# Softmax sums of 32 attention heads in PE column tiles, their inverses replicated by DMA, and three heads woven in the source

## Chip, cores and metric

The kernel runs on one core of one Trainium2 chip. The time is device microseconds (us) of one execution; each kernel is executed several times and the median is quoted, with the lowest and highest. TensorE's mean granted clock was 0.978 to 0.985 unless another value is given. TensorE is called PE below, VectorE DVE, ScalarE ACT, GpSimd POOL.

## The reference, cut to what matters

Four layers follow one another: A, B, A, B. Layer A is a two-dimensional Fourier filter; the change does not touch it. Layer B is attention with a memory: 64 segments of 32 positions, each attending to 8 memory rows and itself, 32 heads of 128, model width 640.

```python
for s in range(n_seg):                                   # 64 segments
    xs = x[:, s * seg_len:(s + 1) * seg_len, :]
    h = jnp.concatenate([mem, xs], axis=1)               # 8 + 32 rows
    q, k, v = (jnp.einsum('btd,dhe->bhte', h, W) for W in (Wq, Wk, Wv))
    scores = jnp.einsum('bhqe,bhke->bhqk', q, k) * scale # masked
    p = softmax(scores)
    o = jnp.einsum('bhte,hed->btd', jnp.einsum('bhqk,bhke->bhqe', p, v), Wo)
    mem = o[:, :M, :]                                    # memory of the next segment
    outs.append(o[:, M:, :])
x = x + _B_ref(_layernorm(x), B_mem0, B_Wq, B_Wk, B_Wv, B_Wo, seg_len)
```

## The kernel before

The kernel guesses the memory of every segment, computes all segments at once, and checks the guess afterwards (a slower pass exists for a failed check; it does not run on these inputs). So layer B is a loop over 32 heads of large matmuls: the projections Q, K, V, then scores, exponentials, sums, values. The queries of a head (2119 columns) are cut into five groups `g_` of at most 502 columns, each with its own PSUM bank. This is the part that the change replaces, shortened with `...`:

```python
def scores(h):
    for i, part in enumerate(st.parts):                  # 9 parts a head
        ps = pa.tile([128, 512], FP32, name="pss", tag="pss")
        ...                                              # K x Q matmuls
        nc.scalar.activation(out=E[:, 0:n], in_=ps[:, 0:n], func=Exp, accum_out=eE[:, i:i + 1])    # L739
        nc.vector.tensor_tensor(out=P[:, o0:o0 + n], in0=E[:, 0:n], in1=bs.mask[...], op=mult)     # L740

def values(h, P):
    for g_ in range(NG):                                 # 5 groups
        psl = pa.tile([128, 512], FP32, name="psl", tag="psl")
        pso = pa.tile([128, 512], FP32, name="pso", tag="pso")
        for dst, lhs in ((psl, ones128), (pso, V of the tile)):
            for ...:                                     # 18 matmuls a head for each of the two, L754
                nc.tensor.matmul(dst[:, lo - q0:hi - q0], lhsT=lhs(t), rhs=P[:, off:off + hi - lo], ...)
        nc.scalar.activation(out=L[:, 0:n], in_=psl[:, 0:n], func=Ln, bias=floor)                  # L758
        nc.scalar.activation(out=R[:, 0:n], in_=L[:, 0:n], func=Exp, scale=-1.0)                   # L759
        nc.gpsimd.tensor_tensor(out=accR[:, 0:n], in0=accR[:, 0:n], in1=R[0:1, 0:n], op=add)       # L760, range check
        nc.vector.tensor_tensor(out=oT[...], in0=pso[...], in1=R[...], op=mult)                    # L765
        nc.vector.tensor_tensor(out=oTm[...], in0=pso[...], in1=R[...], op=mult)                   # L767, memory rows

for h in range(H):
    if h % 2 == 0: w = load_w(h // 2); v_pair(w, h // 2) # V of two heads
    q_all(w, h); k_all(w, h)
    P = scores(h)
    if todo is not None: values(*todo)                   # the head before
    todo = (h, P)
```

The sums multiply the exponentials by a 128x128 matrix of ones, so that every one of 128 partitions holds the sum of a column, where the values need it. A scheduler reorders the instructions of each engine when the kernel is built, so the source order is not quite the order that runs.

Of the kernel before, what the change touches and what calls it, by code (L numbers as in the profile page):

```python
# [9 lines left out]
FP32 = mybir.dt.float32  # L10
# [277 lines left out]
EXP_MAX, INV_MAX, SUM_FLOOR = 2.0 ** 50, 2.0 ** 40, 2.0 ** -60  # L288
# [31 lines left out]
class _Stream:  # L320
# [9 lines left out]
    GS = 15  # L330
# [3 lines left out]
    NQ = PRE + NSEG * SW  # L334
    NM = PRE + NSEG
# [5 lines left out]
    def __init__(self):  # L341
# [16 lines left out]
        qpos[0:PRE] = np.arange(PRE)  # L358
# [32 lines left out]
    def qbase(self, s):  # L391
        return self.PRE + self.SW * s
# [50 lines left out]
def _b_mem_check(tc, g, pj, pc, wk, oTm, mnb, gq_of, NM, NC, flag_col, sums=None):  # L443
# [3 lines left out]
    for c in range(5):  # L447
# [3 lines left out]
        nc.scalar.copy(out=mnb[:, c, :], in_=ps[:, :NM])  # L451
# [18 lines left out]
    accR, accE = sums  # L470
    ne = accE.shape[1]
    okE = wk.tile([128, ne], BF16, name="okE", tag="okE", bufs=1)
    nc.vector.tensor_single_scalar(out=okE[:], in_=accE[:], scalar=EXP_MAX, op=ALU.is_le)
    nc.tensor.matmul(pe2[:, 0:ne], lhsT=ones_c[:, 0:1], rhs=okE[:], start=True, stop=True)
    ok = wk.tile([1, 512 + ne], FP32, name="okq", tag="okq", bufs=1)
    nc.vector.tensor_single_scalar(out=ok[:, 0:512], in_=accR[:], scalar=INV_MAX, op=ALU.is_le)
    nc.vector.tensor_single_scalar(out=ok[:, 512:], in_=pe2[:, 0:ne], scalar=127.5, op=ALU.is_ge)
# [7 lines left out]
def _b_out(tc, g, env, wk, oT_of, psx):  # L485
    nc = tc.nc
    Wo_sb, eps_t = g["Wo_sb"], g["eps"]
    rt = lambda ap: ap.rearrange("(t p) d -> p t d", p=128)
    xs, xd = rt(env["x_src"]), rt(env["x_dst"])
    xnd = rt(env["xn_dst"]) if env["xn_dst"] is not None else None  # L490
    for blk in range(4):
        lhs = oT_of(blk)
        for j in range(4):
            t = 4 * blk + j
            xr = wk.tile([128, D], BF16, name="xr", tag="xr")
            nc.sync.dma_start(out=xr[:], in_=xs[:, t, :])
            xo = wk.tile([128, 1, D], BF16, name="xo", tag="xo")
            for c0, c1 in ((0, 320), (320, D)):
                ps = psx()
                for h in range(H):  # L500
                    nc.tensor.matmul(ps[:, 0:c1 - c0], lhsT=lhs(h, j), rhs=Wo_sb[:, h, c0:c1], start=(h == 0), stop=(h == H - 1))  # L501
                nc.vector.tensor_tensor(out=xo[:, 0, c0:c1], in0=ps[:, 0:c1 - c0], in1=xr[:, c0:c1], op=ALU.add)  # L502
            nc.sync.dma_start(out=xd[:, t, :], in_=xo[:, 0, :])
            if xnd is not None:
                st, mv = _ln_tiles(nc, wk)
                _ln_stats(nc, st, mv, xo[:, 0, :], 0)
                xno = wk.tile([128, 1, D], BF16, name="xno", tag="xno")
                _ln_apply(nc, wk, mv, xo, xno, 1, eps_t, on_dve=True)
                nc.sync.dma_start(out=xnd[:, t, :], in_=xno[:, 0, :])


def _b_full_pass(tc, g, lay, env, flag_col):
# [86 lines left out]
    with octx:  # L599
# [11 lines left out]
        _b_out(tc, g, env, wk, oT_of, lambda: pj.tile([128, 512], FP32, name="psx", tag="pj"))  # L611


def _b_fast_pass(tc, g, bs, env, mnb, flag_col):
# [3 lines left out]
    ones128 = g["ones128"]  # L618
    oTx_d = g["oTx_d"]
    PRE, SW, GS, NG, NT, NQ = st.PRE, st.SW, st.GS, st.NG, st.NT, st.NQ  # L620
# [10 lines left out]
    accR = ap.tile([1, 512], FP32, name="accR")  # L631
    accE = ap.tile([128, len(st.parts)], FP32, name="accE")
    for t in (accR, accE):
        nc.gpsimd.memset(t[:], 0.0)
    with ExitStack() as ctx:
# [4 lines left out]
        oT0 = g["big"].tile([128, H - 2, 512], BF16, name="oT0", tag="big")  # L640
        QTs = [qk.tile([128, NQ + 1], BF16, name=f"QT{i}") for i in range(2)]
        KTs = [qk.tile([128, st.NK], BF16, name=f"KT{i}") for i in range(2)]
        for KT in KTs:
            for a, b in ((502, 512), (1007, 1024), (1519, 1536), (2035, 2048)):
                nc.vector.memset(KT[:, a:b], 0.0)
# [36 lines left out]
        def q_m(w, h):  # L682
            QT = QTs[h % 2]
            ps = pj.tile([128, 512], FP32, name="psq", tag="pj")
            chain(w["Wq"], h % 2, ps[:, 0:PRE], hT, 0, PRE)
            chain(w["Wq"], h % 2, ps[:, PRE:st.NM], gq, 0, NSEG)
            nc.scalar.mul(out=QT[:, 0:PRE], in_=ps[:, 0:PRE], mul=scale)
            nc.scalar.mul(out=x_view(QT, PRE, NSEG)[:, :, SEG], in_=ps[:, PRE:st.NM], mul=scale)

        def q_all(w, h):  # L690
            QT = QTs[h % 2]
            for g_, (lo, hi) in enumerate(kruns):
                ps = pj.tile([128, 512], FP32, name="psq", tag="pj")
                chain(w["Wq"], h % 2, ps[:, 0:hi - lo], hT, lo, hi)
                n = GS if g_ < NG - 1 else 3
                o = st.kbase(g_ * GS) - lo
                qv = x_view(QT, st.qbase(g_ * GS), n)
                nc.scalar.mul(out=qv[:, :, 0:SEG], in_=x_view(ps, o, n)[:, :, 1:SW], mul=scale)  # L698
                if g_ < NG - 1:
                    nc.vector.tensor_scalar_mul(out=qv[:, :, SEG], in0=x_view(ps, o, n)[:, :, 0], scalar1=scale)  # L700
                if g_ == 0:
                    nc.vector.tensor_scalar_mul(out=QT[:, 0:PRE], in0=ps[:, 0:PRE], scalar1=scale)  # L702
                elif g_ == NG - 2:
                    q_tail(QT, ps, SEG - st.TAIL, st.TAILK - lo, st.TAIL)
                elif g_ == NG - 1:
                    nc.vector.tensor_scalar_mul(out=x_view(QT, st.qbase(NSEG - 4), 4)[:, :, SEG], in0=ps[:, 0:3 * SW + 1:SW], scalar1=scale)
                    q_tail(QT, ps, 0, 3 * SW + 1, SEG - st.TAIL)

        def k_all(w, h):
            KT = KTs[h % 2]  # L710
            for lo, hi in kruns:
                ps = pj.tile([128, 512], FP32, name="psk", tag="pj")
                chain(w["Wk"], h % 2, ps[:, 0:hi - lo], hT, lo, hi)
                nc.vector.tensor_copy(out=KT[:, lo:hi], in_=ps[:, 0:hi - lo])

        def v_pair(w, hp):
            V = Vt[hp] = vp.tile([128, NT, 256], BF16, name="V", tag="V")
            for t in range(0, NT, 2):
                n = min(2, NT - t)
                ps = pj.tile([128, 512], FP32, name="psv", tag="pj")  # L720
                for i in range(n):
                    for ch in range(5):
                        nc.tensor.matmul(ps[:, i * 256:(i + 1) * 256], lhsT=hT[:, ch, (t + i) * 128:(t + i + 1) * 128], rhs=w["Wv"][:, ch, :],  # L723
                                         start=(ch == 0), stop=(ch == 4))
                nc.scalar.copy(out=V[:, t:t + n, :].rearrange("p a b -> p (a b)"), in_=ps[:, 0:n * 256])  # L725

        def scores(h):
            QT, KT = QTs[h % 2], KTs[h % 2]
            P = sm.tile([128, st.NP], BF16, name="P", tag="P")
            eE = sm.tile([128, len(st.parts)], FP32, name="eE", tag="eE")  # L730
            for i, part in enumerate(st.parts):
                o0 = st.tiles[part[0]][0][3]
                ps = pa.tile([128, 512], FP32, name="pss", tag="pss")
                for t in part:
                    for _, lo, hi, off in st.tiles[t]:
                        nc.tensor.matmul(ps[:, off - o0:off - o0 + hi - lo], lhsT=KT[:, t * 128:(t + 1) * 128], rhs=QT[:, lo:hi], start=True, stop=True)  # L736
                        n = off - o0 + hi - lo
                E = sm.tile([128, 512], BF16, name="E", tag="E")
                nc.scalar.activation(out=E[:, 0:n], in_=ps[:, 0:n], func=ACTF.Exp, accum_out=eE[:, i:i + 1])  # L739
                nc.vector.tensor_tensor(out=P[:, o0:o0 + n], in0=E[:, 0:n], in1=bs.mask[:, o0:o0 + n], op=ALU.mult)  # L740
            nc.gpsimd.tensor_tensor(out=accE[:], in0=accE[:], in1=eE[:], op=ALU.add)
            return P

        def values(h, P):
            V = Vt[h // 2]
            oT = oTs.tile([128, st.NX], BF16, name="oT", tag="oT")
            for g_ in range(NG):
                q0, n = st.q0[g_], st.q0[g_ + 1] - st.q0[g_]
                mine = [(t, r) for t in range(NT) for r in st.tiles[t] if r[0] == g_]
                psl = pa.tile([128, 512], FP32, name="psl", tag="psl")  # L750
                pso = pa.tile([128, 512], FP32, name="pso", tag="pso")
                for dst, lhs in ((psl, lambda t: ones128[:]), (pso, lambda t: V[:, t, (h % 2) * 128:(h % 2 + 1) * 128])):
                    for i, (t, (_, lo, hi, off)) in enumerate(mine):
# [319 lines left out]
```

## Time and profile before

| | before |
|---|---|
| time (median; lowest to highest) | 1904.98 us (1903.92 to 1905.18), 3 runs |
| head loop, from the first matmul of the guess to the last dense projection | 608 us a layer |
| of that: useful steps of PE other than sums | 506 us |
| of that: sums | 31 us |
| of that: waits | 71 us |
| tail, from there to the last output projection | 157 us a layer |

The last rows are my own accounting from the trace. I take the time between the starts of two neighbouring matmuls as what the first one cost. For every form of matmul I take a short step as its work and call the rest wait, filed under the pair of neighbours. For the column-tiled sums, "sums" is the whole of their steps plus what the matmul just before them costs more than usual. The loops of both layers agree within 2 us in all kernels but two, for which both values are given.

The engines of the kernel before, from the page: busy us, share of the span, number of instructions.

```profile
span 1903.3 us, 38101 instructions
PE 1743.0 (92%) x14586; PEld 1183.3 (62%) x14587; DVE 906.0 (48%) x2786; ACT 1006.3 (53%) x2844; POOL 384.4 (20%) x436
```

PE is the bound, the rest have room on average. The windows view shows the same inside the first head loop; the columns are the window, its length, busy us of PE, PEld (weight loads), DVE, ACT and POOL, PE's clock, the DMA share and GB/s.

```profile
212.00:795.00 583.00, 551.23 (x4567) 367.77 (x4565) 296.51 (x952) 406.11 (x1222) 171.08 (x183) 1.00 0.17 59
300.00:720.00 420.00, 397.67 (x3282) 264.25 (x3281) 216.02 (x700) 295.05 (x889) 126.27 (x135) 1.00 0.19 64
```

Four sums in the loop of the kernel before take 0.24 us, some 60 ns each, from 415.60 to the next matmul (start, length, engine, line, operation; neighbouring matmuls of one kind are merged, xcount; the lengths overlap):

```profile
415.35 0.41 PE L754 MATMUL pso<-P,V 128*128 128x139 bf16 x4
415.60 0.40 PE L754 MATMUL psl<-P,ones_72 128*128 128x132 bf16 x4
415.84 0.40 PE L754 MATMUL pso<-P,V 128*128 128x132 bf16 x4
```

What PE waits for in the head loops of the kernel before, from the view of waits (total us, times, longest):

```profile
PE psl L754 <- ACT L L758: 32.6, 62, 0.7
PE pso L754 <- DVE oTmf L767: 18.8, 34, 1.0
```

The sums wait for the Ln that empties their bank (both layers together), the values for the multiply that empties theirs. And the groups of instructions that the change touches, from the page (busy us, mean ns of one, then the idle time before them and what ended it):

```profile
L760 POOL TENSOR_TENSOR accR<-accR,R 1x495 f32<-1x495 f32 (+2 forms) x320 | 343.6, 1074 | 700.1 <-ACT R L759 689.9
L740 DVE TENSOR_TENSOR P<-E,maskf 128x269 bf16<-128x269 bf16 (+5 forms) x576 | 178.9, 326 | 51.8 <-ACT E L739 37.7
L758 ACT ACTIVATE L<-psl,floor 128x495 f32<-128x495 f32 (+2 forms) x320 | 195.5, 627 | 7.3 <-PE psl L754 7.3
L759 ACT ACTIVATE R<-L 128x495 f32<-128x495 f32 (+2 forms) x320 | 180.3, 577 | 5.5 <-POOL accR L760 2.4
L739 ACT ACTIVATION_READ_ACCUMULATOR E<-pss 128x1 f32 x576 | 123.0, 214 | 0.0
```

### The profile page before, as it was taken

The page shows a single profiled execution, that of the slowest core. Times are in us where ns is not written, and L with a number is a line of the kernel's source. Part 1 is how long each engine was busy: PE and PEld are TensorE (multiplying, and loading weights), DVE is VectorE, ACT ScalarE, POOL GpSimd, SP SyncE. Part 2 cuts the span into 40 slices and gives each one's busy share as a digit, 9 for nine tenths or more (in the row PEclk, how much of TensorE's full clock was granted, in tenths as well). Part 3 has the DMA queues.
Part 4 walks back from the last instruction along what each step waited for, and adds up shares of the span by engine and source line. Part 5 has one row for each costly group of instructions (what it writes and reads, how often), then busy time and mean ns, then how long its engine had stood idle before and what let it go on. Part 6 is the DMA issues. An engine that isn't in the chain of part 4 may idle for free. (4 is left out here: it accounts for less than half of the span.)

```text
span 1903.3 us, 38101 instructions
## 1 busy us (share of the span) xinstructions
PE 1743.0 (92%) x14586; PEld 1183.3 (62%) x14587; DVE 906.0 (48%) x2786; ACT 1006.3 (53%) x2844; POOL 384.4 (20%) x436
## 2 busy tenths in 40 slices
PE   4987999999999999899969879999999999998998
PEld 3655666666666666667746556666666666665775
DVE  5656244554555455533345653455455545545111
ACT  4334476776677666710033445677767766676000
POOL 0100032232233222400000001223323322232000
PEclk8998999999999999999989989999999999999999
DMA  5753011212122111164163621121112111212430
GB/s 133 193 207 125 23 55 62 71 53 73 44 73 73 51 66 48 36 208 143 53 165 73 228 91 33 51 72 63 62 55 73 62 62 53 70 46 80 147 125 30
DMA packets 138169, 163.21 MB, mean 86 GB/s; under 512 B 7136, under 2 KB 118000, under 8 KB 136432
## 3 DMA queue, kind: packets, MB, share of 16 engines
q1 hardware_dynamic: 131776, 133.74, 21.2%
q0 software_dynamic: 6192, 26.86, 5.5%
q8 instruction: 118, 1.93, 0.4%
q14 instruction: 83, 0.68, 0.1%
HBM read 121.86 MB, written 49.81 MB: 90 GB/s over the span
## 5 line engine op out<-in xcount | busy, mean ns | idle before, releaser
L760 POOL TENSOR_TENSOR accR<-accR,R 1x495 f32<-1x495 f32 (+2 forms) x320 | 343.6, 1074 | 700.1 <-ACT R L759 689.9
L723 PE MATMUL psv<-wWv,hTf 128*128 128x256 bf16 x2720 | 334.5, 272 | 5.1 <-DVE hTf L901 2.4
L739 ACT ACTIVATE E<-pss 128x269 bf16<-128x269 f32 (+5 forms) x576 | 216.9, 390 | 206.1 <-PE pss L736 178.6
L657 PE MATMUL psq<-hTf,wWq 128*128 128x128 bf16 (+3 forms) x1560 | 304.8, 335 | 2.6 <-ACT QT_2048 L675 0.4
L657 PE MATMUL psk<-hTf,wWk 128*128 128x495 bf16 (+3 forms) x1600 | 303.8, 342 | 0.0
L723 PEld LDWEIGHTS <-hTf 128*128 128x128 bf16 x2720 | 256.9, 97 | 40.3 <-issue 6.3
L657 PEld LDWEIGHTS <-wWk 128*128 128x128 bf16 x1600 | 144.4, 97 | 146.2 <-issue 10.6
L765 DVE TENSOR_TENSOR oT<-pso,R 128x480 bf16<-128x480 f32 (+1 forms) x320 | 185.8, 581 | 80.0 <-ACT R L759 60.5
L657 PEld LDWEIGHTS <-wWq 128*128 128x128 bf16 x1580 | 134.2, 97 | 122.3 <-DVE QT_25578 L702 5.7
L740 DVE TENSOR_TENSOR P<-E,maskf 128x269 bf16<-128x269 bf16 (+5 forms) x576 | 178.9, 326 | 51.8 <-ACT E L739 37.7
L501 PE MATMUL psx<-Wo_sb,oTxl 128*128 128x320 bf16 x1440 | 203.4, 299 | 0.0
L725 ACT CAST V<-psv 128x512 bf16<-128x512 f32 (+1 forms) x288 | 165.7, 580 | 65.0 <-PE psv L723 65.0
L758 ACT ACTIVATE L<-psl,floor 128x495 f32<-128x495 f32 (+2 forms) x320 | 195.5, 627 | 7.3 <-PE psl L754 7.3
L759 ACT ACTIVATE R<-L 128x495 f32<-128x495 f32 (+2 forms) x320 | 180.3, 577 | 5.5 <-POOL accR L760 2.4
L501 PEld LDWEIGHTS <-oTxl 128*128 128x128 bf16 x1440 | 140.9, 98 | 54.7
L754 PE MATMUL psl<-P,ones_72 128*128 128x132 bf16 (+8 forms) x1152 | 133.7, 218 | 42.9 <-ACT L L758 32.6
L754 PE MATMUL pso<-P,V 128*128 128x132 bf16 (+8 forms) x1152 | 118.8, 219 | 19.5 <-DVE oTmf L767 18.8
L739 ACT ACTIVATION_READ_ACCUMULATOR E<-pss 128x1 f32 x576 | 123.0, 214 | 0.0
L502 DVE TENSOR_TENSOR xo<-psx,xr 128x320 bf16<-128x320 f32 x64 | 31.5, 491 | 189.8 <-PE psx L501 189.8
L754 PEld LDWEIGHTS <-ones_72 128*128 128x128 bf16 x1152 | 86.8, 97 | 46.1 <-issue 43.5
L754 PEld LDWEIGHTS <-V 128*128 128x128 bf16 x1152 | 81.8, 98 | 36.1 <-issue 23.6
L700 DVE TENSOR_SCALAR QT_25578<-psq 128x15 bf16<-128x15 f32 x60 | 13.2, 221 | 157.7 <-ACT QT_25578 L698 157.7
(638 smaller groups left out, 2065.1 us busy)
## 6 DMA issues: line engine op xcount, KB each, us to landing
oTx_d<-oT SPq DMA_DIRECT2D x60, 512.0 KB, 2.6
oTxl<-oTx_d SPq DMA_DIRECT2D x18, 1024.0 KB, 7.8
Wv_sb<-in_B_Wv_dram POOLq DMA_DIRECT2D x10, 1024.0 KB, 9.6
wWq<-in_B_Wq_dram SPq DMA_DIRECT2D x32, 320.0 KB, 3.3
wWk<-in_B_Wk_dram SPq DMA_DIRECT2D x32, 320.0 KB, 3.1
wWv<-in_B_Wv_dram SPq DMA_DIRECT2D x32, 320.0 KB, 3.1
Wo_sb<-in_B_Wo_dram POOLq DMA_DIRECT2D x4, 1280.0 KB, 7.8
oTxl<-oTx_d SPq DMA_DIRECT2D x6, 768.0 KB, 5.8
```

Source lines behind the costliest of these rows:

```text
L501: nc.tensor.matmul(ps[:, 0:c1 - c0], lhsT=lhs(h, j), rhs=Wo_sb[:, h, c0:c1], start=(h == 0), stop=(h == H - 1))
L502: nc.vector.tensor_tensor(out=xo[:, 0, c0:c1], in0=ps[:, 0:c1 - c0], in1=xr[:, c0:c1], op=ALU.add)
L657: nc.tensor.matmul(ps, lhsT=w[:, ch, hh * 128:(hh + 1) * 128], rhs=src[:, ch, lo:hi], start=(ch == 0), stop=(ch == 4))
L723: nc.tensor.matmul(ps[:, i * 256:(i + 1) * 256], lhsT=hT[:, ch, (t + i) * 128:(t + i + 1) * 128], rhs=w["Wv"][:, ch, :], start=(ch == 0), ...
L725: nc.scalar.copy(out=V[:, t:t + n, :].rearrange("p a b -> p (a b)"), in_=ps[:, 0:n * 256])
L739: nc.scalar.activation(out=E[:, 0:n], in_=ps[:, 0:n], func=ACTF.Exp, accum_out=eE[:, i:i + 1])
L740: nc.vector.tensor_tensor(out=P[:, o0:o0 + n], in0=E[:, 0:n], in1=bs.mask[:, o0:o0 + n], op=ALU.mult)
L754: nc.tensor.matmul(dst[:, lo - q0:hi - q0], lhsT=lhs(t), rhs=P[:, off:off + hi - lo], start=(i == 0), stop=(i == len(mine) - 1), skip_grou ...
L758: nc.scalar.activation(out=L[:, 0:n], in_=psl[:, 0:n], func=ACTF.Ln, bias=g["floor"][:, 0:1])
L759: nc.scalar.activation(out=R[:, 0:n], in_=L[:, 0:n], func=ACTF.Exp, scale=-1.0)
L760: nc.gpsimd.tensor_tensor(out=accR[:, 0:n], in0=accR[:, 0:n], in1=R[0:1, 0:n], op=ALU.add)
L765: nc.vector.tensor_tensor(out=oT[:, s0 * SEG:(s0 + ns) * SEG].rearrange("p (s t) -> p s t", t=SEG), in0=v(pso)[:, :, 0:SEG], in1=v(R)[:, : ...
```

## The change

The intent has three parts.

1. Sums. The ones matrix shrinks from 128 to 32 columns, and the matmuls of four groups go to four column tiles of the array, side by side. The sums of groups 0 to 3 then lie in partitions 0, 32, 64 and 96 of one bank; Ln and Exp run once a head over 634 columns instead of five times over up to 502 columns. As the inverses are no longer replicated over all partitions, they are stored in DRAM and loaded back as a broadcast to 128 partitions.
2. The range check adds `R` and the sums of every head into accumulators on POOL, on 128 partitions; the accumulator reads of ACT go.
3. Weave. The source interleaves the projections of head h with the scores of head h-1 and the values of head h-2, and starts three output accumulations before the last heads are done.

```diff
+        def sums(h, P):
+            psl = pa.tile([128, 2, 512], FP32, name="psl", tag="psl", bufs=1)
+            for i in range(max(len(r) for r in runs)):
+                for g_ in range(NG):
+                    ...
+                    b, j = divmod(g_, 4)
+                    nc.tensor.matmul(psl[32 * j:32 * j + 32, b, ...], lhsT=ones32[:], rhs=P[:, off:off + hi - lo], ...)   # L767
+            nc.scalar.copy(out=sums_sb[:, 0:GQ], in_=psl[:, 0, 0:GQ])
+            nc.scalar.copy(out=sums_sb[0:32, GQ:GQ + NL], in_=psl[0:32, 1, 0:NL])
+            nc.scalar.activation(out=R[:], in_=sums_sb[:], func=ACTF.Ln, bias=g["floor"][:, 0:1])
+            nc.scalar.activation(out=R[:], in_=R[:], func=ACTF.Exp, scale=-1.0)                                          # L772
+            Rd = g["dram"].tile([1, NQ], FP32, name="Rd", tag="Rd", bufs=3)
+            nc.sync.dma_start(out=Rd[0:1, 0:4 * GQ]..., in_=R[0:128:32, 0:GQ])                                           # L774
+            nc.sync.dma_start(out=Rd[0:1, 4 * GQ:NQ], in_=R[0:1, GQ:GQ + NL])                                            # L775
+            Rb = Rbs2[h % 2]
+            nc.sync.dma_start(out=Rb, in_=Rd[0:1, :].to_broadcast([128, NQ]))                                            # L777
+            nc.gpsimd.tensor_tensor(out=accR[:], in0=accR[:], in1=R[:], op=ALU.add)                                      # L778
+            nc.gpsimd.tensor_tensor(out=accS[:], in0=accS[:], in1=sums_sb[:], op=ALU.add)                                # L779
+            return Rb
 ...
-                nc.scalar.activation(out=E[:, 0:n], in_=ps[:, 0:n], func=ACTF.Exp, accum_out=eE[:, i:i + 1])
+            nc.scalar.activation(out=E[:, 0:n], in_=ps[:, 0:n], func=ACTF.Exp)
 ...
-                nc.scalar.activation(out=L[:, 0:n], in_=psl[:, 0:n], func=ACTF.Ln, bias=g["floor"][:, 0:1])
-                nc.scalar.activation(out=R[:, 0:n], in_=L[:, 0:n], func=ACTF.Exp, scale=-1.0)
-                nc.gpsimd.tensor_tensor(out=accR[:, 0:n], in0=accR[:, 0:n], in1=R[0:1, 0:n], op=ALU.add)
 ...
+        def merge(dense, dep):          # dense matmuls, with the dependent ones spread evenly between them
+            n = 0
+            for i, f in enumerate(dense):
+                f()
+                while n * len(dense) < (i + 1) * len(dep):
+                    dep[n]()
+                    n += 1
 ...
+        for h in range(H + 2):
+            ...                         # dense: Q and K of head h, half of V of a pair; for h >= H: begin(), an early output
+            if 1 <= h <= H:
+                dep += [lambda part=part: score_part(h - 1, P[h - 1], part) for part in st.parts]
+            if h >= 2:
+                dep += [lambda g_=g_: value_group(h - 2, P[h - 2], Rb[h - 2], oT[h - 2], g_) for g_ in range(NG)]
+            merge(dense, dep)
+            if 1 <= h <= H:
+                Rb[h - 1] = sums(h - 1, P[h - 1])
+            if h >= 2:
+                store(h - 2, oT[h - 2])
```

## The prediction

> **What bounds it now.** TensorE. The page gives it 92% busy at a granted clock of 0.98; DVE (48%), ACT (53%) and POOL (20%) do not limit on average. By windows, the two head loops (32 heads each; 212–795 us and 1152–1738 us) take 583 and 586 us, 61% of the span. Only the loops and their ends change.
>
> Inside one loop I split TensorE's time by start-to-start steps of its matmuls in the trace: V projection 162 us (median step 109 ns, so 148 us if nothing waited), K 143, Q 138, sums 61, values 46, scores 33. Sums and values each have 576 matmuls with a median step near 60 ns, i.e. about 34 us of work apiece. So roughly 530 us of the 584 is work and about 54 us per layer is waiting. The view of waits names it: sums wait for the Ln that empties their PSUM bank (32.6 us), values for the multiply behind the inverses (18.8 us).
>
> **What the change does.**
> - Sums: 18 matmuls a head with 32 columns of ones, four column tiles side by side. The Trainium skill ("TensorE: Matmul & The Clock Gate", packing small matmuls) gives 2.38x for three column tiles at 512 columns; "TensorEngine Tiling (Array Packing)" says a mode switch drains the engine and column tiling disables fast weight load. No trace here shows either yet. The built order has the sums in about three bursts, so six switches a head. Estimate: 1.05 us a head becomes 0.6–0.9 us: 5–15 us per layer.
> - ACT per head: five Ln and five Exp (5.9 us) become two copies, one Ln, one Exp on 634 columns (about 2.5 us, estimated from 0.69 and 0.64 us for 495 columns); the accumulator reads (1.9 us) go.
> - Values lag two heads and no longer wait for Ln and Exp of their own group.
> - New latency: copies, Ln, Exp (about 3 us with queueing), a small store (about 2.5 us), then a 1.08 MB broadcast load each head. 1 MB loads land in 7.8 us here, so about 13–14 us from last sum to inverses. In the built order Q and K of a head and half of V (12–14 us) stand between. That is close: some heads may wait 0–1 us. DMA share in the loop rises from 0.17 to about 0.35.
> - Three output accumulations start before the last heads finish, filling the bubble at the loop's end (about 4–5 us idle per layer).
>
> **On the critical path.** Per layer: waits fall from 54 to about 18 us, sums save about 9, tail 4: about 49 us, 98 for both.
>
> **Predicted: 1807 us, range 1765 to 1858.** Chances: faster by over 2% 0.92, within 2% 0.06, slower 0.02.
>
> **What would show each step.** Right: loops of about 537 us; no TensorE wait on Ln; sums matmuls stepping under 45 ns on average; ACT busy under 800 us; broadcast landing in 7–10 us; few waits of the output multiply on that DMA; shorter gap before the first output projection. Wrong: column sums stepping 60 ns or more, or gaps at the switches; multiplies waiting on the broadcast, with value matmuls stalled behind PSUM; Q/K/V steps above 209/109 ns.
>
> **What would make it wrong.** The broadcast taking over 12 us stalls every head: up to 1–2 us x 64, eating the gain. Large switch costs would cancel the sums' gain. If the weave removes nearly all waiting, 1765 us or below.

## The result

| | before | after |
|---|---|---|
| time (median; lowest to highest) | 1904.45 us (1903.86 to 1905.18), 4 runs | 1843.01 us (1841.55 to 1846.57), 4 runs |
| ratio after / before | | 0.968 (95%: 0.9663 to 0.9697) |
| granted clock | 0.981 | 0.981 |
| head loop a layer | 608 | 580 |
| useful steps other than sums | 506 | 507 |
| sums | 31.1 | 33.7 |
| waits | 71 | 40 |
| tail a layer | 157.3 | 154.8 |

Ratios here and below are the mean time of one kernel's runs over that of the other's of the same rounds, so they are not quite the ratios of the medians quoted. The change is faster by 61 us: (28 + 2.5) us in each of two layers. I had expected 97 to 98. The direction was right and the range held, but the gain was two thirds of the expected one.

The engines after, and the inner window of the first loop, with the same columns as before:

```profile
span 1841.2 us, 36901 instructions
PE 1709.3 (93%) x14778; PEld 1149.3 (62%) x14779; DVE 938.2 (51%) x2792; ACT 793.7 (43%) x1874; POOL 222.5 (12%) x180
```

```profile
300.00:720.00 420.00, 402.99 (x3505) 264.65 (x3505) 238.41 (x731) 232.49 (x576) 73.54 (x48) 1.00 0.36 125
```

ACT lost 213 us and POOL 162 us, neither of which bounded anything. PE's busy share of the same 420 us rose from 397.67 to 402.99 us: only 5 us less idle. The page has the groups that answer to those before:

```profile
L755 DVE TENSOR_TENSOR P<-E,maskf 128x269 bf16<-128x269 bf16 (+5 forms) x576 | 221.2, 389 | 65.0 <-ACT E L754 49.7
L779 POOL TENSOR_TENSOR accS<-accS,sums_sb 128x634 f32<-128x634 f32 x64 | 98.2, 1534 | 998.5 <-ACT sums_sb L770 998.5
L778 POOL TENSOR_TENSOR accR<-accR,R 128x634 f32<-128x634 f32 x64 | 97.9, 1529 | 27.4 <-ACT R L772 25.9
```

The masked product of DVE (L740 before, L755 after) is the same instruction on the same tiles, and yet its mean went from 326 to 389 ns. The view of waits after shows a new name at the top of the loop's waits:

```profile
PE psq L678 <- DVE QT_2047 L721: 13.7, 15, 1.0
PE psq L678 <- DVE QT_25002 L721: 13.7, 15, 1.0
PE pso L787 <- DVE oTmf L793: 6.9, 11, 1.1
```

The waits on Ln are gone: no line of this view names it in the loops. In their place the Q projection waits 15 times a layer, 0.9 us each, for a DVE instruction that empties a Q bank. The two findings belong together, as the timeline of one such wait shows (start us, length us, engine, line, operation; in brackets the idle time before it and what ended that):

```profile
431.88 1.53 POOL L778 TENSOR_TENSOR accR<-accR,R 128x634 f32<-128x634 f32 x1 [0.45 <-ACT R L772]
431.93 0.57 ACT L719 ACTIVATE QT_2047<-psq 128x480 bf16<-128x480 f32 x1
432.07 1.50 DVE L755 TENSOR_TENSOR P<-E,maskf 128x283 bf16<-128x283 bf16 x1 [0.68 <-ACT E L754]
...
433.50 0.21 DVE L721 TENSOR_SCALAR QT_2047<-psq 128x15 bf16<-128x15 f32 x1
433.58 0.28 DVE L755 TENSOR_TENSOR P<-E,maskf 128x267 bf16<-128x267 bf16 x1
...
433.76 1.00 PE L678 MATMUL psq<-hTf,wWq 128*128 128x499 bf16 x4 [0.96 <-DVE QT_2047 L721]
```

POOL's add runs from 431.88 to 433.41. DVE starts a product at 432.07 and ends it at 433.57, 0.16 us after the add; the next product, of nearly the same size and with no add running, takes 0.28 us. Behind the long product stands the 0.21 us read of the Q bank, and behind that PE, idle for 0.96 us. In the whole trace 60 of the 576 products take over 500 ns (up to 1506 ns), and all 60 started while one of these adds ran and ended 152 to 166 ns after its end. The Trainium skill ("SBUF — State Buffer", section "Who interferes with whom") says that a DVE instruction with two SBUF inputs contends with a GpSimd instruction that reads SBUF, and that the shared ports are an exclusive lock. The trace agrees, with 1.5 us beside it: the product ends only after the add has. A control lies in the kernel before: 36 multiplies of DVE with one input in PSUM and one in SBUF (L765, 128x480) started while an add of POOL ran, and took 648 ns in the median, against 656 ns for all of them.

The second finding is in the sums. A piece of PE's timeline of the kernel after, at the last heads of the first loop (neighbouring equal matmuls are merged, xcount):

```profile
756.40 0.23 PE L767 MATMUL psl<-P,ones_72 128*32 128x132 bf16 x1
756.66 0.27 PE L751 MATMUL pss<-QT_2046,KT_2048 128*128 128x141 bf16 x2
756.86 0.23 PE L767 MATMUL psl<-P,ones_72 128*32 128x132 bf16 x1
757.02 2.28 PE L678 MATMUL psk<-hTf,wWk 128*128 128x502 bf16 x10
...
761.93 0.36 PE L767 MATMUL psl<-P,ones_72 128*32 128x132 bf16 x12
762.22 0.32 PE L751 MATMUL pss<-QT_2047,KT_2049 128*128 128x132 bf16 x3
```

Twelve column-tile matmuls in a row occupy 0.29 us from the start of the first to the next matmul of another kind; a single one occupies 0.26 us (756.40 to 756.66). Start to start, two sums in different column tiles stand 3 to 4 ns apart (the skill's page "TensorE: Matmul & The Clock Gate", Part 3, gives about 4 ns per tile: this agrees). But a matmul before a burst costs some 92 ns more than otherwise, and the last one of the burst steps 150 to 268 ns before a full-array matmul starts. The built order has three bursts a head, a burst being a run of sums with no other matmul between them (93 bursts for the 31 heads whose sums lie inside the loop). The skill ("TensorEngine Tiling (Array Packing)", Key Properties) says that a change of tiling mode drains the engine and gives no figure; here a change in and out comes to about 0.27 us for a burst. Whether that is a drain, or weight loads that no longer overlap, no run separates: before the matmul at 756.66 a weight load of 95 ns stands in the open, before the one at 757.02 it does not. The sums of a layer cost 33.7 us, the whole of their steps plus what the matmul just before them costs more than usual, against 31.1 us with the full array: the column tiles saved nothing.

The broadcast was as near as I had feared. From the end of Exp (L772) to the landing took about 9 us in the middle of the loop: 2.8 us until the broadcast is issued, 1.8 us until its first packet moves, 4.2 us of packets for 1.08 MB (these sum to 8.8). The first multiply of a head starts a median 0.45 to 0.5 us after the landing, so it is often that transfer that it waits for.

### The profile page after: what moved, and what is told of

The parts are those of the page before. It is cut to its first block, busy times and chain, and to the rows that moved or that the text cites. A ratio compares the mean times of both kernels' runs of the same rounds, so it can differ in the third digit from the quotient of the medians. Undisturbed runs are those within 1.5% of the kernel's fastest.

```text
span 1841.2 us, 36901 instructions
## 1 busy us (share of the span) xinstructions
PE 1709.3 (93%) x14778; PEld 1149.3 (62%) x14779; DVE 938.2 (51%) x2792; ACT 793.7 (43%) x1874; POOL 222.5 (12%) x180
## 5 line engine op out<-in xcount | busy, mean ns | idle before, releaser
L678 PE MATMUL psk<-hTf,wWk 128*128 128x495 bf16 (+3 forms) x1600 | 317.2, 342 | 0.5 <-DVE hTf L961 0.3
L755 DVE TENSOR_TENSOR P<-E,maskf 128x269 bf16<-128x269 bf16 (+5 forms) x576 | 221.2, 389 | 65.0 <-ACT E L754 49.7
L779 POOL TENSOR_TENSOR accS<-accS,sums_sb 128x634 f32<-128x634 f32 x64 | 98.2, 1534 | 998.5 <-ACT sums_sb L770 998.5
L516 DVE TENSOR_TENSOR xo<-psx,xr 128x320 bf16<-128x320 f32 x64 | 31.3, 490 | 175.2 <-PE psx L502 175.2
L791 DVE TENSOR_TENSOR oT<-pso,Rb 128x480 bf16<-128x480 f32 (+1 forms) x160 | 92.9, 581 | 53.3 <-PE pso L787 39.9
L787 PEld LDWEIGHTS <-V 128*128 128x128 bf16 x1216 | 92.7, 98 | 14.5 <-issue 8.2
L778 POOL TENSOR_TENSOR accR<-accR,R 128x634 f32<-128x634 f32 x64 | 97.9, 1529 | 27.4 <-ACT R L772 25.9
L199 PEld LDWEIGHTS <-YT 128*128 128x128 bf16 x640 | 63.1, 99 | 27.1 <-DVE wi L76 2.2
L249 PE MATMUL psg<-GT,UT 128*128 128x320 bf16 x384 | 67.3, 312 | 1.8 <-ACT UT L222 1.8
L250 ACT CAST G<-psg 128x640 bf16<-128x640 f32 x64 | 44.3, 692 | 52.4 <-PE psg L249 49.6
L791 DVE TENSOR_TENSOR oT<-pso,oT_2044 128x480 bf16<-128x480 f32 (+1 forms) x80 | 46.5, 581 | 37.1 <-PE pso L787 29.0
```

The costliest lines, as they stand in the source:

```text
L199: nc.tensor.matmul(ps[:, cout, 0:NF], lhsT=lhsT, rhs=Fd[:, ch, FD_IDX[(cin, cout)], :], start=(n == 0), stop=(n == 9))
L249: nc.tensor.matmul(psg[:, i, 0:320], lhsT=lhsT, rhs=Gd[:, ch, i * 320:(i + 1) * 320], start=(ch == 0), stop=(ch == 2))
L678: nc.tensor.matmul(ps, lhsT=w[:, ch, hh * 128:(hh + 1) * 128], rhs=src[:, ch, lo:hi], start=(ch == 0), stop=(ch == 4))
L778: nc.gpsimd.tensor_tensor(out=accR[:], in0=accR[:], in1=R[:], op=ALU.add)
L779: nc.gpsimd.tensor_tensor(out=accS[:], in0=accS[:], in1=sums_sb[:], op=ALU.add)
L787: nc.tensor.matmul(pso[:, lo - q0:hi - q0], lhsT=V[:, t, (h % 2) * 128:(h % 2 + 1) * 128], rhs=P[:, off:off + hi - lo], start=(i == 0), st ...
```

## The experiments

My theory after the first look: of the missing 36 us, most are (S) mode switches of the sums and (P) POOL's adds blocking DVE. Rivals: (D) the broadcast is late, (W) the weave is worth less than I thought, (T) the tail. Twelve kernels ran. Accounting per layer, as above (where the layers differ, both are given):

| run | median us | ratio to before (95%) | loop | sums (bursts) | waits | tail |
|---|---|---|---|---|---|---|
| after | 1843.0 | 0.9680 (0.9663–0.9697) | 580 | 33.7 (93) | 40 | 154.8 |
| weave only | 1875.4 | 0.9847 (0.9831–0.9863) | 594 | 31.3 | 56 | 156.6 |
| sums only | 1938.3 | 1.0177 (1.0160–1.0194) | 620 | 57 (184) | 55 | 165 |
| no POOL adds | 1809.9 | 0.9502 (0.9486–0.9518) | 565, 562 | 33.8 (93) | 24, 21 | 154.6 |
| one burst a head | 1815.1 | 0.9530 (0.9514–0.9546) | 566 | 16.5 (30) | 42 | 155 |
| both mended | 1791.8 | 0.9415 (0.9402–0.9427) | 556 | 16.5 (30) | 32 | 153.5 |
| DMA once | 1858.5 | 0.9766 (0.9752–0.9779) | 588 | 24.4 (65) | 57 | 154.6 |
| no early output | 1867.0 | 0.9805 (0.9791–0.9818) | 580 | 33.7 (93) | 39 | 167 |
| sums only, one burst | 1909.8 | 1.0030 (1.0015–1.0045) | 602 | 17.2 (31) | 78 | 166 |
| broadcast twice | 2005.7 | 1.0541 (1.0524–1.0557) | 656, 644 | 21–22 (44) | 126, 115 | 163 |
| broadcast for two heads only | 1773.7 | 0.9314 (0.9302–0.9327) | 550.5 | 16.5 (30) | 27 | 151.5 |
| sums copied on DVE | 1804.4 | 0.9466 (0.9452–0.9481) | 562 | 16.5 (30) | 38 | 153.6 |
| inverses in bf16 | 1800.2 | 0.9448 (0.9428–0.9468) | 561.5 | 16.5 (30) | 37.5 | 151.6 |

The kernel before measured 1903.75 to 1904.9 us. The granted clock was lower in four of the runs: 0.974 to 0.979 (sums only), 0.972 to 0.976 (no early output), 0.972 to 0.975 (sums only, one burst) and 0.947 to 0.953 (broadcast twice). The 57 us of the sums-only run hold some 5 us in which sums wait for products of DVE (10.2 us for both layers in the view of waits); without these, its sums cost 52 us. The letters of the theories in the expectations are not always mine: their theory B is S here, and S in the first of them is something else. The useful steps were 506 to 508 us a layer in the kernels whose split is used in the argument; so a loop's differences are sums and waits. Every run passed the comparison with the reference. The two whose inverses are stale on purpose passed as well, so the tolerance does not see which head an inverse came from.

### The weave alone

The sums, Ln, Exp and accumulators of the kernel before, in the woven order of the kernel after. The edit, abridged and partly in words:

```diff
-    psl[32*j:32*j+32, b, ...] <- ones32; 2 copies, 1 Ln, 1 Exp; store and broadcast; 2 POOL adds on 128x634
+    for g_ in range(NG): psl[:, ...] <- ones128; Ln; Exp into Rb[:, q0:q0+n]; POOL add on one row
+    Exp of the scores with accum_out, POOL add of eE
```

> The woven loop and the early output accumulation of the changed kernel, but the sums as before: 128 columns of ones, five Ln and five Exp a head, the accumulators of exp read, no replication by DMA. If the weave is what gained (theory W), this comes out near the changed kernel: 1840 to 1860 us, with little waiting for Ln. If the gain needed the shorter work on ScalarE (theory S: one Ln and one Exp a head instead of five each), the waits of sums for Ln stay and it comes out at 1870 to 1900 us. I expect about 1875 us.

It measured 1875.4 us: 29 us saved, nearly all of it in the loops (608 to 594), with 15 us less waiting a layer, although all five Ln and Exp remain. So the order of the work alone is worth about half of the change's gain. That the number came out as expected is luck: I had expected waits of sums for Ln to stay, and the view of waits shows none. Merging Ln and Exp is thus not needed to remove them; the order does it. The sums here wait for products instead (10.1 us for both layers). Its products suffer too: 120 of 576 took over 500 ns.

### The sums alone

The new sums and broadcast in the old order: V of the pair first, then Q, K, scores, sums, values of the head before.

```diff
-            merge(dense, dep)
-            Rb[h - 1] = sums(h - 1, P[h - 1])
+            q, k, scores of h;  Rb[h] = sums(h, P[h])
+            if h:
+                values(h - 1)
```

> The column-tiled sums, one Ln and one Exp a head and the replication by DMA, but the loop in the order of before: no weave, no early output. If column tiles save matmul time (theory C), 1840 to 1860 us. If every burst of sums costs about 0.3 us in switches in and out (theory B, from the steps of the changed kernel: 92 ns in, 150 to 268 ns out, 3 to 4 ns between tiles), the six or so bursts a head in this built order cost 1.8 us a head against 1.05 us for sums before, so about 45 us more in all, while waits for Ln (about 50 us in all) go: about 1895 us, range 1870 to 1915.

It measured 1938.3 us, 34 us slower than before and above the expected range. Theory C is refuted. Its built order has six bursts a head (184 in a loop), and the sums took 57 us a layer (52 without their waits for products), 21 to 26 more than with the full array. The largest wait of the loop is another one:

```profile
PE psk L678 <- ACT QT L685: 53.3, 60, 0.9
```

The K projection waits 60 times for ACT to empty a Q bank. The tail is 8 us longer than before; in it stands one wait of some 8.5 us before the values of the last head, as long as the way of the inverses through DRAM. The two parts alone sum to +5 us (-29 and +34), the whole is -61 us: the parts depend on one another, and no single part "gave" the 61 us.

### No adds on POOL

```diff
-            nc.gpsimd.tensor_tensor(out=accR[:], in0=accR[:], in1=R[:], op=ALU.add)
-            nc.gpsimd.tensor_tensor(out=accS[:], in0=accS[:], in1=sums_sb[:], op=ALU.add)
```

This makes the range check empty; the outputs are unaffected.

> The changed kernel without the two 128x634 adds on POOL in each head (the range check on sums then passes always; the output stays right). The built order of TensorE is the same. Theory P: the 26 us per layer that Q matmuls wait come from a DVE product of two SBUF operands that stands 1.2 us behind such an add, and delays the DVE read of a Q bank; then the waits before Q fall to under 10 us per layer and the time to 1800 to 1820 us. Theory D: the remaining waits come from the broadcast DMA; then the time stays within 5 us of 1843 us.

It measured 1809.9 us, 33 us less than the kernel after. In the first B layer, compared matmul for matmul, PE's order is that of the kernel after, so little else changed. The page's line of the product:

```profile
L755 DVE TENSOR_TENSOR P<-E,maskf 128x269 bf16<-128x269 bf16 (+5 forms) x576 | 165.6, 289 | 59.9 <-ACT E L754 43.9
```

Its mean fell from 389 to 289 ns, none took longer than 313 ns, and the waits of PE before a Q matmul fell from 26 to 6 us a layer; that is 40 of both layers, and the time fell by 33. Theory P holds: the mechanism and its size. (The kernel before had 34 such products, up to 919 ns, from its adds on a single row.)

### One burst a head

The ones are made for every head from the last product of that head, so that no sum can start before it is done, and the scheduler cannot pull the early ones forward.

```diff
+            ones_h = sm.tile([128, 32], BF16, name="ones_h", tag="ones_h")
+            nc.vector.tensor_scalar(out=ones_h[:], in0=P[:, st.NP - 32:st.NP], scalar1=0.0, scalar2=1.0, op0=ALU.mult, op1=ALU.add)
-                    nc.tensor.matmul(..., lhsT=ones32[:], ...)
+                    nc.tensor.matmul(..., lhsT=ones_h[:], ...)
```

> The changed kernel with its sums forced into one burst a head: the stationary ones are written anew for each head by a small DVE operation that reads the last columns of that head's products, so no sum can start before all products are there. Theory B: 32 bursts per layer instead of 93, each 0.3 us, so sums fall from 33.6 us per layer to about 15 us and the time to about 1807 us (1800 to 1820), unless a wait at the burst eats some of it. If switches are hidden or free, the time stays within 5 us of 1843 us.

It measured 1815.1 us, 28 us less than the kernel after. The bursts fell from 93 to 30 and the sums from 33.7 to 16.5 us a layer, with the same matmuls. Waits did not fall (40 and 42 us). The loop's order changed elsewhere too, so it is the sums' own figure that tests the theory, more than the 28 us: (33.7 - 16.5) / 63 bursts = 0.27 us a burst. (The loop of this kernel holds the sums of 30 heads, not 31, which explains some 0.5 us of the difference.) The line 8.3 us + 0.27 us for each burst gives 16.4, 25.9, 33.4 and 58 us for 30, 65, 93 and 184 bursts, where 16.5, 24.4, 33.7 and, without waits for products, 52 us were measured; from 93 to 184 bursts the slope is 0.20 us. Theory S holds, at 0.2 to 0.27 us a burst.

### Both mended

The single burst, and a range check without POOL: the inverses of all heads stay in DRAM, one row a head, and are compared once, at the layer's end.

```diff
-    accR = ap.tile([128, GQ + NL], FP32, name="accR")
-    accS = ap.tile([128, GQ + NL], FP32, name="accS")
+    Rdk = g["dram"].tile([H, NQ], FP32, name="Rdk", tag="Rdk", bufs=2)
 ...
-            Rd = g["dram"].tile([1, NQ], FP32, name="Rd", tag="Rd", bufs=3)
+            Rd = Rdk[h:h + 1, :]
-            nc.gpsimd.tensor_tensor(out=accR[:], ...)        # both adds
 ...                                                          # in the check:
+    nc.sync.dma_start(out=Rk[:], in_=sums[:])                # [32, 2119]
+    nc.vector.tensor_single_scalar(out=okw[:], in_=Rk[:], scalar=INV_MAX, op=ALU.is_le)
+    nc.vector.tensor_single_scalar(out=okw[:], in_=Rk[:], scalar=1.0 / SUM_MAX, op=ALU.is_ge)
```

> A candidate for a better version: one burst of sums a head, and no adds on POOL. Its range check stays real: the inverses of all heads, which go to DRAM anyway, are kept there and compared once at the end of the layer. If theories B (switches) and P (POOL adds that stall DVE products) are about separate costs, the gains add: 33 us and 28 us off 1843 us give about 1782 us, range 1772 to 1795. If both were the same wait seen twice, it stays near 1805 us.

It measured 1791.8 us, 51 us less than the kernel after, less than the 61 us of the two repairs added, and the check is a real one. It is the fastest version here that computes what it should, at 0.9415 of before. PE's timeline at a head shows the one burst left:

```profile
418.79 0.53 PE L769 MATMUL psl<-P,ones_h 128*32 128x132 bf16 x19
419.25 2.28 PE L678 MATMUL psq<-hTf,wWq 128*128 128x502 bf16 x10
```

All 19 matmuls of the head's sums (the woven order has one more than the old) occupy 0.46 us, from 418.79 to 419.25; with the switch in, the mean is 16.5 / 30 = 0.55 us a head, where the full array took 31.1 / 31 = 1.0 us. My estimate was 0.6 to 0.9 us a head: too cautious for an unbroken burst, too hopeful for a broken one (33.7 / 31 = 1.09).

### The broadcast: DMA only for the first two heads of the layer

```diff
-            nc.sync.dma_start(...)                            # 2 stores and the broadcast, every head
+            if h < 2:
+                nc.sync.dma_start(...)                        # later heads use stale inverses: wrong on purpose
```

> The changed kernel with the inverses replicated by DMA for the first two heads only, later heads use those again (the result is wrong on purpose; times of the other steps do not depend on values). Theory D (the broadcast DMA, its latency or its 68 MB of traffic, costs time): 20 us or more below 1843 us. Theory of enough slack: the trace shows only some 10 waits of over 1 us on that DMA and PSUM waits behind them of about 3 us a layer, so 1833 to 1842 us.

It measured 1858.5 us, 15 us slower than the kernel after, with less work. That was no answer, and neither expected range was met: with the DMA dependency gone, the scheduler built another order. 60 products stand behind an add of POOL in both kernels, but here it is nearly always the product in front of the read of a Q bank.

```profile
PE psq L678 <- DVE QT L721: 54.6, 59, 1.0
```

This wait doubled (27.4 us before, both layers), in 59 places instead of 30. The run is another witness for theory P and says nothing of D.

### No early output

```diff
-                dense += [begin] * (1 if h == H else 2)
+                dense += [lambda: None]
```

> The changed kernel without the three output accumulations that start before the last heads finish. They should fill the bubble at the end of each layer's head loop: without them about 4 us more a layer, 1851 us (1846 to 1858). If the bubble was filled by the memory check anyway, within 2 us of 1843 us.

It measured 1867.0 us. The loops and their waits are the same as in the kernel after; the tail is 167 us instead of 154.8. So the early output is worth 12 us a layer, three times the 4 us that I had put on it, and the time lies above the expected range. But against the kernel before (157.3) the tail gained only 2.5 us: without the early output the new tail is 10 us longer than the old one, and the early output takes that back. The two runs with the new sums and without the weave, which have no early output either, have nearly the same tail, 165 to 166 us. The trace of this run shows where the time goes: one wait of PE before values, 7.8 us from start to start in each layer.

```profile
777.81 1.52 POOL L778 TENSOR_TENSOR accR<-accR,R 128x634 f32<-128x634 f32 x1
...
779.36 0.49 DVE L476 TENSOR_SCALAR okw<-accR 128x634 f32<-128x634 f32 x1 [4.54 <-POOL accR L778]
...
781.26 0.82 DVE L479 TENSOR_REDUCE ok<-okw 128x1 bf16<-128x634 f32 x1
781.99 0.65 DVE L791 TENSOR_TENSOR oT<-pso,oT 128x480 bf16<-128x480 f32 x1
...
782.77 1.25 PE L787 MATMUL pso<-P,V 128*128 128x132 bf16 x8 [7.62 <-DVE oTmf L793]
```

The values wait for a bank that DVE's multiply of the head before the last must empty. By the DMA records the inverses of that head landed at 779.23 us. But in DVE's order the range check stands in front of the multiply; it waits for POOL's add of the last head, until 779.33 us, and takes 2.7 us itself. So the way through DRAM and the range check share this wait. In the sums-only kernels, in contrast, the multiply comes right behind the landing (822.59 and 823.07 us), so there the inverses end the wait. The wait is not all. Beginning inside it, the trace shows a granted clock of 0.5, from 777.9 to 791.5 us (1699.5 to 1716.5 us in the other layer). The sums-only kernels have such a stretch there too; the kernel after has none from its head loop to the end of its tail. Runs of eight value matmuls took 1.07 to 1.27 us in this stretch, against 0.75 us at the full clock in the sums-only kernel. So part of the 12 us is the wait, some 7 us longer than the longest of the tail with the early output, and the rest, at least in part, is the slower clock.

### The sums alone, in one burst

The sums-only kernel with the `ones_h` of above.

> The kernel of the second run (new sums, loop order of before) with its sums forced into one burst a head. Theory B: 184 bursts per layer become about 64 or fewer, each worth 0.3 us, so sums fall from 55 to about 17 us per layer and the time from 1938 us to 1860 to 1880 us, below the kernel before: the sums part was a loss because of its bursts. If its loss came from its 31 us of waits before K (the inverse chain on ScalarE ahead of the Q evacuation) alone, it stays above 1920 us.

It measured 1909.8 us, 28.5 us less than with six bursts, and level with before. The sums cost 17.2 us a layer, 14 less than before, but waits are up from 71 to 78 us and the tail is 9 us longer. Neither expectation was met: the sums fell as theory B said, the time did not. The waits are again those of the sums-only kernel, led by this one:

```profile
PE psk L678 <- ACT QT L685: 43.7, 59, 0.9
```

In the old order K waits for ACT to empty the banks of Q. In one head of the trace (409.6 to 413.3 us) ACT's copies, Ln and Exp of the new sums, 2.4 us, stand among these reads of Q, so the chain of the inverses on ACT, which the expectation named, has a part in it; how large a part, no run separates. So the mended sums alone are worth nothing, and the weave alone 29 us. Late inverses are the smaller part: DVE waits 18 us for the broadcast, both layers together.

### The broadcast twice

From here on the base is the kernel with both mended. A second, unused broadcast of the same size goes to DRAM ahead of the real one.

```diff
+            Rx = g["dram"].tile([128, NQ], FP32, name="Rx", tag="Rx", bufs=2)
+            nc.sync.dma_start(out=Rx[:], in_=Rd[0:1, :].to_broadcast([128, NQ]))
             nc.sync.dma_start(out=Rb, in_=Rd[0:1, :].to_broadcast([128, NQ]))
```

> The mended kernel of the fifth run (1791.8 us) with the 1.08 MB broadcast of inverses issued twice a head, the first time into spare memory, so that its traffic and its time in the queue double. The compiler's order moves the values a little later to fit. Theory D (the broadcast's latency or traffic limits): some 4 us more a head for part of the heads, 1840 us or more. Theory of slack: under 10 us slower, 1790 to 1802 us.

It measured 2005.7 us, 214 us slower than its base, at a granted clock of 0.953 (0.982 in the base); no run here separates what the clock adds. From the end of Exp to the landing now took 13.3 us, with 8.95 us of packets. What PE and DVE wait for, in this kernel:

```profile
PE pso L789 <- DVE oTmf L795: 138.7, 61, 5.2
```

```profile
DVE oT L793 <- DMA Rb<-Rdk: 159.7, 31, 7.9
DVE oT L793 <- DMA oT<-Rdk: 150.2, 32, 8.8
```

DVE's multiply waits 310 us for the inverses, in 63 of 64 heads, and the value matmuls behind it for PSUM. My view that the broadcast had slack is refuted: 4 us more are paid for the most part in every head (214 / 64 = 3.3 us a head, with the lower clock in it, and with another built order: 44 bursts of sums instead of 30). The broadcast of the mended kernel has less than these 4 us of slack.

### The broadcast for the first two heads only

Stores and check stay, so that the rest of the dependencies is kept. Its output is wrong, which doesn't matter for the time.

```diff
+            if h < 2:
                 nc.sync.dma_start(out=Rb, in_=Rd[0:1, :].to_broadcast([128, NQ]))
```

> The mended kernel of the fifth run with the broadcast made for the first two heads only (the result is wrong on purpose; all sums, inverses and their stores to DRAM stay). Like the sixth run, but without the POOL adds, which that run moved in front of a DVE product in every head instead of every second one. Theory D: 20 us or more below 1791.8 us. Theory of slack: 1783 to 1795 us.

It measured 1773.7 us, 18 us less than its base: 5.5 us a layer in the loop, all of it waits, 2 in the tail, and the rest outside of what I split. It lies between the two expected ranges. So the broadcast costs about 18 us in the mended kernel, if the built order, which changes with the dependencies, does not itself make a part of the difference; no run separates the two.

### The sums copied on DVE

To get the inverses earlier, DVE instead of ACT copies the sums out of PSUM.

```diff
-            nc.scalar.copy(out=sums_sb[:, 0:GQ], in_=psl[:, 0, 0:GQ])
+            nc.vector.tensor_copy(out=sums_sb[:, 0:GQ], in_=psl[:, 0, 0:GQ])
```

> A further try for a better version: the mended kernel with the two copies of sums out of PSUM moved from ScalarE to VectorE, which shortens the queue of ScalarE work (copies, Ln, Exp, 2.4 us) that stands before the evacuation of the first Q banks. If the waits of scores and Q there (about 16 us a layer) come from that queue, 10 to 20 us faster: 1772 to 1782 us. If VectorE's own queue takes the copies late, no gain: 1788 to 1796 us.

It measured 1804.4 us, 13 us slower than its base. The inverses came later, not earlier: DVE's waits for the broadcast rose from 20.5 to 44 us, and PE waited longer a layer at two places: 8 us between V and values, and 12.5 us between values and scores (8.7 in the base). What holds the copies up on DVE I did not trace.

### The inverses in bfloat16

This halves the bytes of store and broadcast.

```diff
-    Rdk = g["dram"].tile([H, NQ], FP32, name="Rdk", tag="Rdk", bufs=2)
+    Rdk = g["dram"].tile([H, NQ], BF16, name="Rdk", tag="Rdk", bufs=2)
```

> The mended kernel (1791.8 us) with the inverses written, stored and broadcast in bf16 instead of f32, so that the broadcast moves half the bytes (0.54 MB a head). It is both a test of the DMA's share and a candidate. The first multiply now starts 0.45 us after the landing, and without the broadcast of most heads the time was 1773.7 us. If the transfer's length counts, about 2 us less from Exp to landing and 1775 to 1786 us. If only its fixed latency counts, 1787 to 1793 us. The result must stay correct: the inverse loses what the bf16 product loses anyway.

It measured 1800.2 us (1793.65 to 1803.78), 8 us slower than its base, in spite of half the bytes. The time from the end of Exp to the landing fell from 8.3 to 6.5 us, as expected, DVE's waits for the broadcast fell to 16 us, and the tail by 2 us. But two waits that the base hardly has, of scores for the exponentials (13.2 us) and of K for the evacuation of its banks (7.8 us), came in with a new built order. Whether fewer bytes help the time was not tested cleanly, and it stays open: each edit of the transfer changes the order that the scheduler builds.

## Why the prediction was right or wrong

The prediction was 1807 us and the result 1843: faster by over 2%, as expected with a chance of 0.92, and inside the range. Point by point:

- *What bounds it: TensorE in the two head loops, waiting on Ln and on the multiply.* Right. The 32.6 us of waits on Ln are gone from the profile after, and the 18.8 us on the multiply fell to 6.9 us, each for both layers together. The weave alone saved 15 us of waits a layer, and with the five Ln and Exp left as they were its trace has no wait on Ln: it is the order that removed these waits, not the shorter work on ACT.
- *ACT under 800 us.* Right: 793.7; the copies, Ln and Exp of a head take 2.4 us, where I had estimated 2.5.
- *Loops of about 537 us.* Wrong: that was some 46 us off each loop, and 28 came.
- *"sums save about 9" per layer.* Wrong, and the largest miss: they cost 2.6 us more (33.7 against 31.1), 11.6 us a layer short of the prediction. I named the mode switch and the three bursts, but put no number on it; 0.27 us a burst, 93 bursts, is 25 us. My sign for success, steps of the sums under 45 ns on average, was met (25.0 us / 584 = 43 ns) and misled, because some 92 ns of every burst fall on the matmul before it. The speed-up itself is there: with one burst the sums save 14.6 us a layer.
- *"waits fall from 54 to about 18 us".* Half right. My later, stricter accounting over the whole loop gives 71 to 40: 31 saved instead of 36. Of what is left, 26 us a layer stand before Q, and 20 of them vanish when POOL's adds are taken away. The step of the prediction that failed is one that I did not write: I took the two adds a head on POOL to be harmless, since POOL was idle 80% of the time. They were not: 60 products of DVE took up to 1.5 us behind these adds instead of 0.3 us.
- *"tail 4".* It was 2.5, as a sum of two larger terms: 10 us lost at the loop's end, where the inverses of the last heads, the range check and a stretch of half clock come together, 12 us won by the early output.
- *Broadcast in 7 to 10 us; "some heads may wait 0–1 us".* About right: some 6 us from issue to landing, just under the range, and 9 us from Exp. The danger I named ("over 12 us stalls every head") was shown in kind by doubling it: 13.3 us from Exp to landing, and a wait in 63 of 64 heads.
- *The sum.* Short by 11.6 (sums) + 5 (waits) + 1.5 (tail) = 18 us a layer, 36 in all, which is the 97 predicted less the 61 measured. With both repairs the change saves 112 us, more than I had predicted: 14.6 + 39 + 3.8 us a layer, less 1 us of other steps.

What stays open: of the 32 us a layer of waits in the mended kernel, how much is the broadcast. It is some 7.5 us a layer by the run that has no broadcast after the second head (5.5 in the loop, 2 in the tail), but that run and the experiments that should have split it changed the built order as well. Open too is how the 0.27 us of a burst divide between a drain and weight loads.

## What to carry to other kernels

The column tiles cost more than the full array here in three bursts a head, and half as much in one; look at the built order, not at the source, and give the scheduler a dependency that forces the burst. Before you move work to an idle POOL, look for DVE instructions with two SBUF inputs that will run beside it, and what stands behind them. When a new transfer lands just before its use, double it once on purpose: here that told whether it had slack, while removing it showed mostly what the scheduler did with the freedom. Compare the built orders in both cases.

## What the Trainium skill lacked or had wrong

- "TensorEngine Tiling (Array Packing)", Key Properties: says that a change of tiling mode drains the engine, without a size. Here a burst of column tiles amid full-array matmuls cost 0.2 to 0.27 us beyond its own work: some 92 ns before it, 150 to 268 ns from its last matmul to the next full-array one.
- "TensorE: Matmul & The Clock Gate", Part 3: its measured 2.38x for three column tiles says nothing of bursts. Here the same 18 or 19 matmuls a head cost 33.7 us a layer in 93 bursts, 16.5 us in 30, and 31.1 us on the full array.
- "SBUF — State Buffer", "Who interferes with whom": the rule is right, and a duration beside its ratios would help: a POOL add of 128x634 fp32 took 1.53 us, and a DVE product of 128x283 bf16, normally 0.3 us, took up to 1.5 us beside it, in 60 of 576 cases.
- I found no figure on its DMA page for a row of DRAM broadcast to 128 partitions: here 1.08 MB took 4.2 us of packets and about 6 us from issue to landing, at 36% mean DMA share in the loop.
